# Order of state terms, scans and own terms in the first attention items of a fused RWKV-5 and mixture-of-experts kernel

## The chip, the cores and the metric

The kernel runs on one core of one Trainium2 chip, in float32. The metric is the device time in microseconds (us) of one execution; of several runs the median is taken. A core has five engines with instruction queues of their own, each worked off in order: TensorE (PE; its weight loads are listed apart as PEld), VectorE (DVE), ScalarE (ACT), GpSimd (POOL) and SyncE (SP, which here only issues DMAs).

## What is computed

A recurrent attention block feeds a mixture of experts with one expert for each token:

```python
# attention: B=4, H=8, S=768, head size 48
for t in range(S):
    kt, vt, rt = (k[:, :, t], v[:, :, t], r[:, :, t])
    cur = np.einsum('bhd,bhe->bhde', u[None] * kt, vt)
    y[:, :, t] = np.einsum('bhd,bhde->bhe', rt, state + cur)
    state = w[None, :, :, None] * state + np.einsum('bhd,bhe->bhde', kt, vt)
# x = y as (B, S, 384); experts: E=8, hidden 1024
logits = x @ w_gate;  local_gate = sigmoid(x @ w_local)
e = argmax(logits[b, s]) if s == 0 or local_gate[b, s] < 0.5 else prev_e
out[b, s] = softmax(logits[b, s])[e] * (np.maximum(x[b, s] @ w1[e], 0.0) @ w2[e])
```

## The kernel before

The attention is cut into 16 items (n = 0 to 15), each a batch b = n // 4 and a pair of heads; the sequence of an item is cut into six chunks of 128 tokens. Counted from one, the change's "item 4" is n = 3. Within a chunk the output is a masked matrix product; across chunks it goes through a state. An item consists of these steps, each a method of `Attention`:

- `load(n)`: three DMAs on SP's queue (rk: r and k; kv: k and v by token; vT). It is issued three items ahead; rk and vT have four buffers each, kv has five.
- `scale(n)`: POOL makes ke (keys weighted with the decay to the chunk's end), pd (r times k) and, from n = 3 on, rw (r times the decay). The order is pd, ke for n < 3; rw, ke, pd later; ke, rw, pd for n = 4.
- `keys(n)`: DVE makes kw (keys divided by the decay), and rw for n < 3.
- `added(n)` (L253): 20 matmuls write what each chunk adds to the state into T, 240 columns of the PSUM tile mp. There is one T for all items, and mp also serves the router.
- `states(n)` (L259): one DVE scan turns T into the states S.
- `scores(n, g)` (L288): 24 matmuls into one of two PSUM pairs, g = 0 and 1 being halves of the chunks. It returns the DVE step (L290) that multiplies by the mask into am. The pairs are handed out in turn to scores, to `turn` and to the logits.
- `own(n)` (L269): 8 matmuls write each token's own term into the PSUM tile y (one buffer, released when ScalarE has copied the previous item's y to xT, L314), and DVE multiplies it by vT (L273).
- `inside(n)` (L297) adds the masked products to y, `before(n)` (L310) adds the states' terms and copies y out.
- `turn(n)` (L323, L325) transposes xT into the token layout x; behind the last pair of heads of a batch x is stored to DRAM (L328), for the experts' gathers.

Everything is under a schedule written out by hand: `run` emits the steps in the order in which each engine works them off. Iteration n emits the inside and state terms of item n - 1. For n = 1 and 2 it then emits the scores of item n, both halves, then own, added and states. From n = 5 on the scores run one item ahead (`ahead = n + 1`), n = 4 does its own and those of n = 5. Added and states of item n come early in iteration n, for n = 4 on; for n = 3 they come at the end of its own iteration:

```python
self.scores(ahead, 0)()
keep = self.scores(ahead, 1)
# n == 3, shortened to what it runs
self.own(n)
self.added(3)
keep()
self.states(3)
```

The router of the experts works on two groups of two batches. Its steps for group 0 are laid between the items: with g = 8, `experts_of` in n = 9, `keys` and `runs` (transpose of the key into mp, scan over it) in n = 10, `turn_runs`, `last` and `one_hot` in n = 11, `counts` and `ranks` in n = 12, `slots` in n = 13. Those for group 1 lie between the hidden blocks of the first expert (`Experts.routing`). `one_hot` makes the expert's index ei[:, 1] and, with a shift by 9 on DVE (L720), its multiple of 512 in ei[:, 2], which `slots` adds (L780). The weights of the first expert are fetched on SP's queue in n = 14 (`fetch`, L1039 and L1041), behind all loads of the attention.

Of the kernel before, what the change touches and what calls it, by code (L numbers as in the profile page):

```python
# [11 lines left out]
F32 = mybir.dt.float32  # L12
I32 = mybir.dt.int32
# [7 lines left out]
P = 128  # L21
# [11 lines left out]
ST = 4  # L33
# [28 lines left out]
class Attention:  # L62
# [254 lines left out]
    def turn(self, n, banks):  # L317

        nc, b, h0 = self.nc, self.items[n]["b"], 2 * self.items[n]["hp"]
        xT, x = self.xTs[b], self.xs[b]  # L320
        for h in range(2):
            for c2 in range(C2):
                nc.tensor.transpose(banks[h][:, c2 * P:c2 * P + U], xT[:U, h0 + h, c2 * P:(c2 + 1) * P], self.ident[:U, :U])  # L323
        for h in range(2):
            nc.scalar.copy(x[:, :, (h0 + h) * DH:(h0 + h + 1) * DH],  # L325
                           banks[h][:, :C2 * P].rearrange("p (c e) -> p c e", e=DP)[..., :DH])
        if h0 == H - 2:
            nc.scalar.dma_start(out=self.x_d[b * S:(b + 1) * S, :].rearrange("(c p) d -> p c d", p=P), in_=x)  # L328

    def logits(self, b, bank):  # L330

# [13 lines left out]
    def run(self, router, fetch, heads):  # L345
# [11 lines left out]
        for n in range(M + 1):  # L357
            if n + AHEAD - 1 < M:
                self.load(n + AHEAD - 1)
            elif n + 2 == M:  # L360
                fetch()
            if n == 0:
                self.scale(0)
                self.keys(0)
                self.tables()
                self.scores(0, 0)()
                self.scores(0, 1)()
                self.own(0)
                self.nc.scalar.copy(self.first, self.tab[:, 1, 0])
                self.turn_ends(slice(1, HP))  # L370
                self.warm(3)
                self.added(0)
                self.reciprocals(1)
                self.states(0)
                self.scale(1)
                continue
            if n < 3:

                self.keys(n)
                self.inside(n - 1)  # L380
                self.before(n - 1)
                if n == 2:
                    self.turn(0, pair("tp"))
                self.nc.scalar.copy(self.first, self.tab[:, n + 1, 0])
                self.scores(n, 0)()
                keep = self.scores(n, 1)
                self.own(n)
                keep()
                self.added(n)
                self.states(n)  # L390
                if n == 1:
                    self.reciprocals(2)
                self.scale(n + 1)
                continue
            if n < M:
                self.turn(n - 2, pair("tp"))
                if n == 3:
                    self.reciprocals(3)
                if n < 5:
                    self.keys(n)  # L400
                if n > 3:
                    self.added(n)
                    self.states(n)
            if n == 4:
# [24 lines left out]
            self.before(n - 1)  # L429
            if n == 6:  # L430
                router.cast()
            if n == M:
                break
            if n == g + 3:
                router.last(0, mp[:, mp_end:])
                router.one_hot(0, (0,))
            if n == g + 7:

                router.summed(0, 0)
                router.copied(0, self.nc.vector.tensor_copy)  # L440
                router.head(pair("tb")[0])
                heads()

            ahead = n if n < 5 else n + 1
            if ahead < M:
                self.scores(ahead, 0)()
                keep = self.scores(ahead, 1)
            if n % HP == 0:

                keep()  # L450
                self.own(n)
                self.logits(n // HP - 1, pair("lp")[0])
                if n == 4:
                    self.scores(5, 0)()
                    self.scores(5, 1)()
                    self.keys(6)
                if n == g + 4:
                    router.counts(0, [mp, mp[:, E * NC // 2:]])
                    router.ranks(0, (0,))
                if n > 4:  # L460
                    self.keys(n + 2)
                if n == g + 4:
                    router.ranks(0, (1,))
            else:
                self.own(n)
                if n == g + 2:
                    router.keys(0, mp)
                    router.runs(0)
                if n == 3:
                    self.added(3)  # L470
                if 4 < n < M - 2:
                    self.keys(n + 2)
                if ahead < M:
                    keep()
                if n == 3:
                    self.states(3)
            if n == g + 1:
                router.experts_of(0, (1,))
            if n == g + 3:
                router.one_hot(0, (1,))  # L480
            if n == g + 5:
                router.places(0, 0)
            if n == g + 6:
                router.places(0, 1)
# [82 lines left out]
class Router:  # L567
# [27 lines left out]
    def open(self, i, pool):  # L595
        g, c = self.g[i], self.g[i]["nc"]
        for name, shape, dt in (
                ("mx", [P, c], F32), ("eq", [P, c, E], F32), ("k", [P, c], F32), ("key", [P, c], F32),
                ("run", [c, P], F32), ("rn", [P, c], F32), ("inc", [P, c + 1], F32),
                ("ei", [P, 3, c], I32), ("oh", [P, E, c], F32),  # L600
                ("exc", [P, E, c + 1], F32), ("pos", [P, E, c], F32), ("far", [P, EARLY, c], F32),
                ("r", [P, c], F32), ("si", [P, 3, c], I32),
                ("eqv", [P, c, E * ST], F32), ("val", [P, c, E * ST], F32), ("ohq", [P, c, P], F32),
# [105 lines left out]
    def one_hot(self, i, parts=(0, 1)):  # L709
# [7 lines left out]
        if 1 in parts:  # L717
            nc.vector.tensor_tensor(g["oh"], spread(g["ei"][:, 1], 1, E), spread(self.ie, 2, g["nc"]), op=Alu.is_equal)

            nc.vector.tensor_scalar(g["ei"][:, 2], g["ei"][:, 1], 9, None, Alu.arith_shift_left)  # L720

    def counts(self, i, bank):

# [52 lines left out]
    def slots(self, i):  # L776

        nc, g = self.nc, self.g[i]
        nc.vector.tensor_reduce(g["r"], g["pos"].rearrange("p e c -> p c e"), axis=AX.X, op=Alu.add)
        nc.vector.scalar_tensor_tensor(g["si"][:, 0], g["r"], float(ST * P - 1), g["ei"][:, 2], Alu.min, Alu.add)  # L780
        nc.vector.tensor_scalar(g["si"][:, 1], g["si"][:, 0], P - 1, None, Alu.bitwise_and)
        nc.vector.tensor_scalar(g["si"][:, 2], g["si"][:, 0], 7, None, Alu.arith_shift_right)

# [937 lines left out]
```

## Time and profile before

| what | us |
|---|---|
| median of 3 runs (lowest, highest) | 386.14 (385.8, 387.54) |
| the profiled execution | 384.17 |
| its span, first to last instruction | 382.4 |
| granted TensorE clock, mean | 0.995 |

Busy time and DMA by stage of that execution (us, but for the last two columns; the stages are cut near where PE starts the scores of n = 1, 2, 3, 4 and 6, then at the router's first transpose and the first logits of the last batch):

| stage | length | PE | DVE | ACT | POOL | DMA share | GB/s |
|---|---|---|---|---|---|---|---|
| 0 to 14.0 | 14.0 | 12.21 | 10.45 | 5.03 | 10.69 | 0.85 | 312 |
| 14.0 to 20.8 | 6.8 | 6.14 | 6.08 | 1.62 | 4.72 | 1.03 | 410 |
| 20.8 to 27.4 | 6.6 | 6.14 | 5.65 | 2.06 | 5.67 | 1.03 | 413 |
| 27.4 to 34.8 | 7.4 | 5.65 | 5.84 | 1.18 | 7.40 | 1.02 | 408 |
| 34.8 to 44.3 | 9.5 | 9.16 | 6.54 | 2.18 | 9.50 | 1.02 | 411 |
| 44.3 to 75.0 | 30.7 | 30.70 | 24.64 | 9.59 | 28.32 | 0.98 | 359 |
| 75.0 to 111.0 | 36.0 | 32.83 | 28.46 | 9.29 | 20.41 | 0.62 | 220 |
| 111.0 to 382.0 | 271.0 | 264.01 | 161.59 | 76.23 | 63.82 | 0.41 | 145 |

How to read it: a stage whose PE column is shorter than its length has idle PE time; the share of DMA is the mean over 16 DMA engines, and a share at 1 means that all had packets under way throughout. Attention is over at about 111 us; behind it lie the ten blocks of the experts. Lines of the profile are those of the kernel's file: `L253` is the matmul of `added`.

### The profile page before, as it was taken

Reading aid. Unit: us, or ns where it says so; the run is one execution under the profiler, and the core shown is the slowest. Engines: PE = TensorE matmul, PEld = TensorE weight load, DVE = VectorE, ACT = ScalarE, POOL = GpSimd, SP = SyncE. Lnnn points to the kernel's source line nnn. Section 1 sums busy time; section 2 is a strip of 40 time slices with the busy share of each in tenths; the row PEclk is TensorE's granted clock in tenths of the full one; section 3 lists DMA queues with packets and bytes.
Section 4 is the critical chain, followed back from the end, with each engine's and each line's share of the span. In section 5 each row is a group of like instructions: output and inputs, shape, how many; then the busy total and the mean of one; then the engine's idle time right before and its main releaser. Section 6 shows DMA issues by size and latency. Waiting matters only on the chain. (4 is left out here: it accounts for less than half of the span.)

```text
span 382.4 us, 9699 instructions
## 1 busy us (share of the span) xinstructions
PE 366.8 (96%) x3858; PEld 324.6 (85%) x3858; DVE 249.3 (65%) x719; ACT 107.2 (28%) x292; POOL 150.5 (39%) x212
## 2 busy tenths in 40 slices
PE   8998999998999999999999999999999999999992
PEld 7775777786759998999999999999998899899971
DVE  6888678888934746496566857758758758466400
ACT  4131233222222112322322333233234233232210
POOL 7779999787222042311422313212323113012022
PEclk9999999999999999999999999999999999999998
DMA  7999998989216881820561254145246156064011
GB/s 267 410 411 411 404 377 311 372 308 351 100 33 204 319 353 30 315 109 22 207 207 62 54 195 195 53 173 207 76 166 228 37 178 228 12 215 169 2 37 37
DMA packets 17477, 74.97 MB, mean 196 GB/s; under 512 B 2729, under 2 KB 6586, under 8 KB 14864
## 3 DMA queue, kind: packets, MB, share of 16 engines
q1 hardware_dynamic: 10048, 56.89, 39.9%
q0 software_dynamic: 3424, 9.52, 7.4%
q10 hardware_dynamic: 3952, 7.87, 5.7%
q8 instruction: 32, 0.52, 0.5%
q14 instruction: 21, 0.17, 0.1%
HBM read 64.83 MB, written 9.51 MB: 194 GB/s over the span
## 5 line engine op out<-in xcount | busy, mean ns | idle before, releaser
L1278 POOL DMA_INDIRECT out_dram<-yo,sid x27 | 26.6, 987 | 102.4 <-ACT yo L1273 79.0
L1129 PE MATMUL h<-exT,w1t 128*128 128x168 f32 (+4 forms) x240 | 54.9, 327 | 0.0
L1133 DVE TENSOR_TENSOR hT<-h,hs 128x168 f32<-128x168 f32 (+3 forms) x60 | 21.1, 351 | 46.4 <-PE h L1129 30.4
L1052 POOL DMA_INDIRECT xg<-x_d,gid x29 | 31.1, 1074 | 37.4 <-DVE sm L887 17.4
L1129 PEld LDWEIGHTS h<-exT,w1t 128*128 128x128 f32 x240 | 41.6, 190 | 0.3 <-issue 0.3
L1079 PE MATMUL h<-exT,w1t 128*128 128x192 f32 (+1 forms) x192 | 38.2, 337 | 0.0
L1198 PE MATMUL y<-factors,sums 128*128 128x192 f32 x168 | 36.8, 326 | 0.0
L290 DVE TENSOR_TENSOR am<-pair,kept 128x768 f32<-128x768 f32 x32 | 30.0, 951 | 8.3 <-PE pair L288 8.1
L1129 PE MATMUL h<-xs,ws 128*128 128x168 f32 (+4 forms) x144 | 35.2, 326 | 0.0
L221 POOL TENSOR_TENSOR pd<-rk 128x384 f32<-128x384 f32 x32 | 31.4, 1003 | 9.6 <-PE y L269 7.4
L1079 PEld LDWEIGHTS h<-exT,w1t 128*128 128x128 f32 x192 | 32.3, 190 | 1.4 <-issue 0.2
L1129 PEld LDWEIGHTS h<-xs,ws 128*128 128x128 f32 x144 | 25.5, 190 | 4.3 <-ACT hs L1136 1.2
L1198 PEld LDWEIGHTS y<-factors,sums 128*128 128x128 f32 x168 | 28.9, 190 | 0.0
L297 PE MATMUL y<-am,kv 128*64 128x128 f32 x384 | 25.1, 276 | 1.0 <-DVE y L273 1.0
L217 POOL TENSOR_TENSOR ke<-kv,endT 128x288 f32<-128x288 f32 x32 | 24.9, 797 | 1.9 <-POOL rw L234 0.8
L234 POOL TENSOR_TENSOR rw<-rk,tab 128x384 f32<-128x384 f32 x26 | 23.6, 928 | 1.4 <-DMA rk<-in_rk_dram 1.4
L288 PE MATMUL pair<-rw,kw 48*64 48x128 f32 (+1 forms) x768 | 22.6, 249 | 0.8 <-DVE kw L241 0.4
L1198 PE MATMUL y<-w2t,hT 128*128 128x192 f32 x96 | 23.0, 328 | 0.0
L314 ACT COPY xT<-y 128x768 f32<-128x768 f32 (+1 forms) x16 | 12.5, 779 | 37.1 <-PE y L310 37.1
L297 PEld LDWEIGHTS y<-am,kv 128*64 128x64 f32 x384 | 21.1, 137 | 1.9 <-DVE y L273 1.3
L1066 DVE COPY exT<-tp 128x384 f32<-128x384 f32 (+6 forms) x29 | 14.0, 489 | 12.9 <-PE tp L1065 12.6
L288 PEld LDWEIGHTS pair<-rw,kw 48*64 48x64 f32 x768 | 19.4, 133 | 3.0 <-issue 0.9
(280 smaller groups left out, 734.7 us busy)
## 6 DMA issues: line engine op xcount, KB each, us to landing
w1t<-in_w_dram SPq DMA_DIRECT2D x9, 1536.0 KB, 6.6
w2t<-in_w_dram SPq DMA_DIRECT2D x9, 1536.0 KB, 7.2
rk<-in_rk_dram SPq DMA_DIRECT2D x15, 768.0 KB, 8.4
kv<-in_kv_dram SPq DMA_DIRECT2D x16, 584.0 KB, 8.7
vT<-in_vT_dram SPq DMA_DIRECT2D x16, 384.0 KB, 6.7
x_d<-x ACTq DMA_DIRECT2D x4, 1152.0 KB, 9.6
w1t<-in_w_dram ACTq DMA_DIRECT2D x1, 1536.0 KB, 10.6
w2t<-in_w_dram ACTq DMA_DIRECT2D x1, 1536.0 KB, 13.8
```

Source lines behind the costliest of these rows:

```text
L217: nc.gpsimd.tensor_mul(t["ke"][:, p::2], t["k"][:, p::2], spread(self.endT[:, p, hp], 1, C2))
L221: nc.gpsimd.tensor_mul(t["pd"][:, z], t["rT"][:, z], t["kT"][:, z])
L234: engine.tensor_mul(t["rw"][:, z], t["rT"][:, z], spread(pw, 1, z.stop - z.start))
L288: nc.tensor.matmul(sc[f * DP:(f + 1) * DP, h, i, x:], lhsT=t["kw"][q, c, o * DP:(o + 1) * DP], rhs=t["rw"][q, c, x:], start=True, stop=True)
L290: return lambda: nc.vector.tensor_mul(t["am"][:, g], sc, spread(self.kept[:, g:g + 3], 1, 2))
L297: nc.tensor.matmul(t["y"][p * DP:(p + 1) * DP, h, c2 * P:(c2 + 1) * P], lhsT=t["v"][:, (2 * c + h) * DH:(2 * c + h) * DH + DP], rhs=t["am" ...
L1052: self.nc.gpsimd.indirect_dma_start(out=xg[:n], out_offset=None, in_=self.x_d[:rows], in_offset=bass.IndirectOffsetOnAxis(ap=u["gid"][:n, ...
L1079: nc.tensor.matmul(h[:, :n], lhsT=u["w1"][:, m, kk, :], rhs=u["xT"][:, kk, :], start=(kk == 0), stop=(kk == DK - 1))
L1129: nc.tensor.matmul(out, lhsT=a, rhs=b, start=start and k == 0, stop=stop and k == len(terms) - 1, skip_group_check=True)
L1133: nc.vector.tensor_tensor(out, a, b, op=Alu.add)
L1198: return lambda: nc.tensor.matmul(bank[:, x * half:(x + 1) * half], lhsT=a, rhs=b, start=(j == 0 and x == 0), stop=(j == FK // 2 - 1), ski ...
L1278: self.nc.gpsimd.indirect_dma_start(out=out.rearrange("n (h d) -> (n h) d", h=2) if half else out, out_offset=bass.IndirectOffsetOnAxis(ap ...
```

## The change

- In iterations n = 1 and 2, `own(n)` moves between the two halves of the scores; DVE's order (mask, own product, mask) stays as it was.
- Iteration n = 3 gets an ending of its own: added and states of n = 3 first, then the first half of the scores, own, and the second half.
- `added(5)` moves from iteration 5 into iteration 4, between the halves of the scores of n = 5. `added(11)` moves from iteration 11 into iteration 10, behind `own(10)` and ahead of the router's transpose into mp. Their scans (`states`) stay where they were.
- The store of x of batch 2 is issued on SP's queue, not on ScalarE's.
- `one_hot`'s shift on DVE becomes a multiplication by 512 on ScalarE, with a float result eb; `slots` adds eb. This holds for both groups.

```diff
         if h0 == H - 2:
-            nc.scalar.dma_start(out=self.x_d[b * S:(b + 1) * S, :]...
+            (nc.sync if b == 2 else nc.scalar).dma_start(out=self.x_d[b * S:(b + 1) * S, :]...
...
                 self.scores(n, 0)()
-                keep = self.scores(n, 1)
                 self.own(n)
-                keep()
+                self.scores(n, 1)()
                 self.added(n)
                 self.states(n)
...
                 if n > 3:
-                    self.added(n)
+                    if n not in (5, g + 3):
+                        self.added(n)
                     self.states(n)
...
             ahead = n if n < 5 else n + 1
+            if n == 3:
+                self.added(3)
+                self.states(3)
+                self.scores(3, 0)()
+                self.own(3)
+                self.scores(3, 1)()
+                continue
...
                 if n == 4:
                     self.scores(5, 0)()
+                    self.added(5)
                     self.scores(5, 1)()
...
                 self.own(n)
                 if n == g + 2:
+                    self.added(n + 1)
                     router.keys(0, mp)
                     router.runs(0)
-                if n == 3:
-                    self.added(3)
...
-                if n == 3:
-                    self.states(3)
...
-            nc.vector.tensor_scalar(g["ei"][:, 2], g["ei"][:, 1], 9, None, Alu.arith_shift_left)
+            nc.scalar.activation(g["eb"], g["ei"][:, 1], Act.Copy, scale=float(ST * P))
...
-        nc.vector.scalar_tensor_tensor(g["si"][:, 0], g["r"], float(ST * P - 1), g["ei"][:, 2], Alu.min, Alu.add)
+        nc.vector.scalar_tensor_tensor(g["si"][:, 0], g["r"], float(ST * P - 1), g["eb"], Alu.min, Alu.add)
```

More of the change, by code (lines that the diff above doesn't have):

```diff
@@ L327, in turn @@
         if h0 == H - 2:
-            nc.scalar.dma_start(out=self.x_d[b * S:(b + 1) * S, :].rearrange("(c p) d -> p c d", p=P), in_=x)
+            (nc.sync if b == 2 else nc.scalar).dma_start(out=self.x_d[b * S:(b + 1) * S, :].rearrange("(c p) d -> p c d", p=P), in_=x)
     def logits(self, b, bank):
@@ L599, in open @@
                 ("run", [c, P], F32), ("rn", [P, c], F32), ("inc", [P, c + 1], F32),
-                ("ei", [P, 3, c], I32), ("oh", [P, E, c], F32),
+                ("ei", [P, 2, c], I32), ("eb", [P, c], F32), ("oh", [P, E, c], F32),
                 ("exc", [P, E, c + 1], F32), ("pos", [P, E, c], F32), ("far", [P, EARLY, c], F32),
```

## The prediction

> **What bounds the kernel now.** I read the page first (busy shares, slices), then the waits of TensorE (PE), then the timelines of PE, VectorE (DVE) and GpSimd (POOL) in the stages that the diff touches. Busy shares, and the head of PE's own waits over the whole span (us in total, times, longest):
>
> ```profile
> PE 366.8 (96%) x3858; PEld 324.6 (85%) x3858; DVE 249.3 (65%) x719; ACT 107.2 (28%) x292; POOL 150.5 (39%) x212
> ```
>
> ```profile
> PE mp L253 <- POOL pd L221: 1.7, 1, 1.7
> PE pair L152 <- POOL ident masks.py:199: 1.5, 1, 1.5
> PE y L297 <- DVE y L273: 1.0, 2, 0.5
> PE mp L253 <- DMA w1t<-in_w_dram: 0.9, 1, 0.9
> PE pair L323 <- DVE am L290: 0.7, 2, 0.3
> ```
>
> PE is the bound; from 111 us on (the experts) no wait of PE at all is listed, so what is won or lost in the attention goes to the end unchanged. The waits listed lie in the attention, and the largest stands in the item that the change rewrites. (The second is the start of the program; the fourth, at 91.31, names a load that lands at 92.4 and isn't read there: the router's sum that reads mp until 91.06 fits better, and the change leaves it.) PE's timeline (start, length, line, tiles, idle before):
>
> ```profile
> 16.23 0.66 PE L253 MATMUL mp<-kv,ke 128*48 128x48 f32 x20
> 17.43 1.95 PE L297 MATMUL y<-am,kv 128*64 128x128 f32 x24 [0.54 <-DVE y L273]
> ...
> 27.43 1.24 PE L288 MATMUL pair<-rw,kw 48*64 48x128 f32 x48 [0.39 <-DVE kw L241]
> ...
> 29.82 0.79 PE L323 MATMUL pair<-ident,xT 112*128 112x112 f32 x6
> 32.34 0.66 PE L253 MATMUL mp<-kv,ke 128*48 128x48 f32 x20 [1.72 <-POOL pd L221]
> 32.79 1.53 PE L297 MATMUL y<-am,kv 128*64 128x128 f32 x24
> ```
>
> and DVE's at the same places:
>
> ```profile
> 16.41 0.97 DVE L273 TENSOR_TENSOR y<-y,vT 128x768 f32<-128x768 f32 x1 [0.49 <-PE y L269]
> ...
> 28.27 0.96 DVE L290 TENSOR_TENSOR am<-pair,kept 128x768 f32<-128x768 f32 x1 [0.66 <-PE pair L288]
> 29.85 0.97 DVE L273 TENSOR_TENSOR y<-y,vT 128x768 f32<-128x768 f32 x1 [0.63 <-PE y L269]
> 30.73 0.95 DVE L290 TENSOR_TENSOR am<-pair,kept 128x768 f32<-128x768 f32 x1
> 31.59 0.64 DVE L259 TENSOR_TENSOR_SCAN S<-step,mp 128x240 f32<-128x240 f32 x1
> ```
>
> Three things are to be seen. The terms of n = 4 (32.34) overwrite T, which the scan of n = 3 (ending 32.23) must have read; the profile names POOL's pd, which ends at 32.25, but the matmuls read only ke and v. So I take the scan as the releaser. Second, that scan is last in a DVE chain (mask, own product, mask, scan) that idles 0.66 + 0.63 us for PE. Third, n = 1 has the same idle piece (0.49) before DVE's own product, and PE pays for it at 17.43.
>
> **A rule of the skill beside the trace.** The Trainium skill, "SBUF — State Buffer", section "Who interferes with whom", says that a DVE tensor_scalar can enter a mode that needs the port pair shared with GpSimd, and then blocks for the whole of a GpSimd instruction that has it. The trace agrees for the shift that the change takes off DVE:
>
> ```profile
> 84.22 1.98 POOL L234 TENSOR_TENSOR rw<-rk,tab 128x384 f32<-128x384 f32 x2
> 85.26 0.97 DVE L720 TENSOR_SCALAR ei<-ei 128x12 int32<-128x12 int32 x1
> 86.15 0.64 DVE L259 TENSOR_TENSOR_SCAN S<-step,mp 128x240 f32<-128x240 f32 x1
> 87.69 1.50 PE L336 MATMUL pair<-xT,wp 128*32 128x384 f32 x16 [0.29 <-DVE am L290]
> ```
>
> Twelve columns take 0.97 us and end with POOL's second rw (86.20); the same shift in the second group takes 0.17 us. The forecast goes by the 0.97.
>
> **Part by part.**
>
> *n = 1 (own terms ahead of the second scores).* Own needs pd (13.75), the first scores (14.85) and y, which ScalarE's copy frees at 14.80. So own runs 14.88 to 15.7 in place of 15.40 to 16.3. The DVE product follows the first mask without idling: 15.83 in place of 16.41, **0.58 us** earlier, and mask, scan, Newton step and keys of n = 2 with it. PE's inside terms (17.43, stretched to 1.95 against 1.5 elsewhere as they wait for the second mask) end at about 18.85, not 19.38: 0.55. If ScalarE's copy came 0.1 late, 0.1 of this goes.
>
> *n = 2.* Same move: own at 21.05 in place of 22.23, product at 22.05 in place of 23.24, and the second mask ends at 23.9, where before inside started at 24.37. Inside then runs 1.5 in place of 1.83. PE finishes its state terms L310 at 26.25, not 27.03: 0.78 in all, 0.2 more than n = 1 gave.
>
> *n = 3.* Now added(3) is first (26.2 to 26.85; ke ready at 24.26), covering the keys' wait (0.39, and the keys are ready at 26.1 anyway). The scan runs 26.95 to 27.6, scores at 26.8, own at 27.5 (pd ready 26.19; y freed 27.1), second scores to 29.05. DVE: first mask 27.65, product 28.5, second mask 29.4 to 30.3. PE: turn(2) to 29.8, added(4) to 30.4 with T long free, inside(3) at 30.4 when the second mask is in. Before: 32.79. The 1.72 us stall goes, and **late next is the second mask**, which PE just meets. Sum up to here: **2.4 us** (0.55 + 0.2 + 1.65).
>
> Does POOL keep up? It runs without a gap from 26.87 (there it waited for kv(4)) and is not moved. PE would want ke(4) at 29.75 (ready 28.43), pd(4) at 33.75 (32.25), rw(5) at 36.0 (34.28), ke(5) at 36.7 (35.80), rw(6) at 42 (39.93). The smallest cover is 0.9 us. Later POOL waits for PE (2.37 us at 70.06), so it has just that much in hand.
>
> *added(5) between the scores of n = 5.* 0.6 us of PE work is moved from behind turn(3) to before it. Turn(3) waited 0.34 us for a bank, and this fills that; but the second scores end at 40.5 (old clock), their mask at 41.5, and the token logits take that mask's bank: they start at 41.57, before 41.55. Gain **0**; from -0.1 to +0.3.
>
> *added(11) behind own(10).* Before, it waited 0.44 us until run's scan (ends 76.59) had read mp, though other columns: the tile is tracked whole. Moved, it runs at 75.1, and inside(10) starts 0.45 sooner. Yet turn_runs then waits for the scan of n = 11 (ends 78.86) at the same 78.92, since DVE is busy without a gap from 70.9. Gain **0**. What it is moved past is the key's transpose, which ends at 76.0; DVE gets to it at 76.19, so 0.2 us of cover; without it, up to 0.4 lost.
>
> *Shift on ScalarE.* For group 0 the scan of n = 12 and the masks after it come 0.9 us sooner; the logits' wait for a bank (0.29, and PE's issue a little) goes, own(12) is late next: **-0.3**. ScalarE is idle there from 80.83 to 82.93; its casts of such a size took 0.2 us. For group 1 ScalarE waits for ei (124.37) with the Relu of the next block queued behind; eb is done at about 124.6 and that Relu started at 124.84: 0, with 0.2 of cover.
>
> *Store of x(2) on SP.* ScalarE loses one DMA issue of 0.38 us at 91.15 and then waits for PE anyway: 0. On SP all loads are out by 83.23, but w1 and w2 of the first expert (83.61, 84.71) now stand behind a store that waits for x(2) at about 88.5. Before, they landed in 8.8 and 12.6 us. 4.3 MB at the 410 GB/s seen early on is 10.4 us, so I estimate landing by 101, against a first use at 112.8 (115.49 before). Twelve us of cover, 0.
>
> **Sum:** -2.4 - 0.3 = **-2.7 us**. The profiled execution took 384.17 (span 382.4, 1.77 outside): 381.5. The three runs' median is 386.14, 2.0 above it; the same difference gives **383.4**. Bounds of the sum: -1.9 (a late copy, 0.3 each for the two moved terms) to -3.2.
>
> **Rivals.**
>
> *B, added(4) is really held by POOL.* The profile names pd, and pd(4) ends 0.09 us before the start. Nowhere does added(n) start before pd(n) ends, so the trace doesn't exclude it. For it: the name. Against: pd is no operand, and own(0) started at 8.99 while ke(0) was still to come, so single POOL instructions do release PE. Then PE stands at 32.3 as before and only the 0.3 is left: **385.8**.
>
> *C, POOL becomes the bound.* If its chain is 1 to 1.5 us later than in the old trace (phases against DVE shift), the head gain is cut to 1.2: **384.9**.
>
> *D, slower.* The loads keep 16 DMA engines wholly busy from 14 to 44 us (share 1.02 at 410 GB/s), and POOL waits for two of them (rk(3) at 21.06, kv(4) at 26.87). Earlier DVE steps free vT and rk sooner, and SP issues the loads of n = 5 and 6 up to 0.8 us sooner, into the same engines, where they could push kv(4) back. PE then stands in order before added(4) and own(4). It decides from kv(4) later by the 1.3 us of cover, and costs more than it brings from 3.7 us (1.3 + 2.4); at 5 us late, **387.1**. Against it: loads of one queue are issued in order, and 0.8 us of transfer is the most that can be pushed in.
>
> **How the numbers follow.** Forecast 0.68, B 0.15, C 0.07, D 0.10. A measurement of this kernel can tell about 0.5% (1.9 us) from no change, so faster is below 384.2. Of the forecast's 0.68 some 0.07 falls above it, of C half below: faster 0.64, within 0.5% 0.26, slower 0.10. The runs spread by 1.7 us, the forecast's own range is 382.4 to 384.5; the range reaches B and below the forecast's best end: 381.9 to 386.2.
>
> **What would show it.** Right: no wait before L253 near 30 us, inside(3) at about 30.4; DVE's product of n = 1 at 15.8; no 0.29 before L336 of n = 12; a new wait of some 0.7 before turn_runs (L700) in place of 0.44 before L253; w1 landing before 102. Wrong: added(4) still at 32.3 (B), waits on POOL between 30 and 45 (C), kv(4) landing after 28 (D), or hidden blocks waiting for w1 or for a Relu queued behind eb.

## The result and the profile after

The changed kernel takes 388.01 us (median of 22 runs, 385.92 to 391.22); the kernel before, run beside it, takes 386.2 (385.05 to 387.78). The ratio is 1.0044, with a 95% interval of 1.0028 to 1.0061. So it is 1.7 us **slower**, where 2.7 us faster had been forecast. Its profiled execution took 389.49 us, 1.5 above that median, with a span of 387.7; that of the kernel before took 384.17, 2.0 below its own (span 382.4). So the two traces lie 5.3 us apart, three times what the medians do, and what they show has to be weighed with that.

The runs fall into two groups by TensorE's mean granted clock. In eight of the 22 it is 0.994 or more, and their median is 386.5; in the other fourteen it is 0.980 to 0.993, and theirs 388.5. Of 218 runs of the kernel before, made beside the experiments, 141 are in the upper group.

Busy time, from the page:

```profile
PE 369.5 (95%) x3858; PEld 327.3 (84%) x3858; DVE 248.8 (64%) x717; ACT 107.4 (28%) x294; POOL 150.6 (39%) x212
```

PE does the same 3858 matmuls and is busy 2.7 us *longer*: that is no wait, but matmuls that ran slowly, 1.7 of it by a stretch at half clock (below). Its waits (us in total, times, longest):

```profile
PE pair L288 <- issue: 4.2, 5, 1.1
PE pair L152 <- POOL ident masks.py:199: 1.5, 1, 1.5
PE mp L253 <- DVE pos L742: 1.2, 1, 1.2
PE mp L705 <- DVE inc L718: 0.9, 1, 0.9
...
PE pair L342 <- DVE am L290: 0.4, 1, 0.4
```

The 1.7 us before `added(4)` and the 0.39 before the scores are gone, as meant. In their place stands a wait that was not there: five pieces, 4.2 us, in the middle of scores, with **no releaser** ("issue": nothing that the profile shows), and a sixth in own(2). PE's timeline of the changed kernel, from own(2) to item 5 (start, length, line, tiles, idle before):

```profile
22.29 0.55 PE L269 MATMUL y<-pd,w_t 48*64 48x384 f32 x4 [0.27 <-issue]
...
27.25 0.66 PE L253 MATMUL mp<-kv,ke 128*48 128x48 f32 x20
27.83 0.44 PE L288 MATMUL pair<-rw,kw 48*64 48x128 f32 x6
28.80 0.60 PE L288 MATMUL pair<-rw,kw 48*64 48x64 f32 x17 [0.53 <-issue]
...
31.31 0.66 PE L253 MATMUL mp<-kv,ke 128*48 128x48 f32 x20
31.80 1.52 PE L297 MATMUL y<-am,kv 128*64 128x128 f32 x24
...
35.20 1.11 PE L288 MATMUL pair<-rw,kw 48*64 48x64 f32 x41 [0.94 <-issue]
...
41.35 0.44 PE L288 MATMUL pair<-rw,kw 48*64 48x128 f32 x8 [1.14 <-issue]
41.72 0.79 PE L323 MATMUL pair<-ident,xT 112*128 112x112 f32 x6
42.95 0.84 PE L342 MATMUL pair<-sel,lT 128*128 128x18 f32 x6 [0.44 <-DVE am L290]
43.73 2.38 PE L297 MATMUL y<-am,kv 128*64 128x128 f32 x24
```

`added(4)` (31.31) no longer stalls and `inside(3)` starts at 31.80, 0.99 before its old 32.79. (This trace is 0.35 late already at the first scores of n = 1; the table under e17 counts from there.) But the scores of n = 4 then stop for 0.94, and those of n = 5, cut apart at 41.35, for 1.14. `inside(4)` at 43.73 is 1.41 *behind* its old 42.32. It also takes 2.38 us in place of 1.53. The stages of that stretch (length; busy us and instructions of PE, PEld, DVE, ACT, POOL; granted clock, DMA share, GB/s):

```profile
40.00:44.00 4.00, 2.42 (x35) 1.87 (x29) 2.23 (x4) 0.87 (x3) 4.00 (x7) 1.00 1.02 411
44.00:48.00 4.00, 4.00 (x74) 3.67 (x74) 0.92 (x20) 0.43 (x2) 3.35 (x7) 0.57 1.03 382
```

PE idles 1.58 us of four, and in the next four the clock is halved (0.57). In the profile of the kernel before PE is busy 3.76 us from 40 to 44, and no slice of the attention has a lowered clock. DVE did what was forecast (compare the timeline of before: mask, product, mask, scan with 0.66 + 0.63 idle):

```profile
27.95 0.65 DVE L259 TENSOR_TENSOR_SCAN S<-step,mp 128x240 f32<-128x240 f32 x1 [0.30 <-PE mp L253]
29.49 0.96 DVE L290 TENSOR_TENSOR am<-pair,kept 128x768 f32<-128x768 f32 x1 [0.89 <-PE pair L288]
30.37 0.95 DVE L273 TENSOR_TENSOR y<-y,vT 128x768 f32<-128x768 f32 x1
31.23 0.94 DVE L290 TENSOR_TENSOR am<-pair,kept 128x768 f32<-128x768 f32 x1
```

The scan is ahead and the chain runs through; only the first mask comes 1.8 us later than forecast (29.49 against 27.65). The scores in front of it start 1.0 later than forecast (27.83 against 26.8), and they stop for 0.53. `added(4)` starts at 31.31, in the middle of POOL's pd(4), so it does not wait for that:

```profile
30.90 1.97 POOL L221 TENSOR_TENSOR pd<-rk 128x384 f32<-128x384 f32 x2
```

The router's stage:

```profile
81.98 0.23 PE L705 MATMUL mp<-ident,run 12*128 12x12 f32 x1 [0.92 <-DVE inc L718]
90.13 0.32 PE L288 MATMUL pair<-rw,kw 48*64 48x128 f32 x4 [0.55 <-issue]
91.14 1.50 PE L336 MATMUL pair<-xT,wp 128*32 128x384 f32 x16
94.98 0.66 PE L253 MATMUL mp<-kv,ke 128*48 128x48 f32 x20 [1.15 <-DVE pos L742]
105.32 0.90 PE L288 MATMUL pair<-rw,kw 48*64 48x128 f32 x31 [1.01 <-issue]
```

The wait before `turn_runs` came (0.92), the logits' 0.29 went, but `added(13)` now waits 1.15 in place of 0.93, and there are two more stops without a releaser. In the experts, 0.9 us more goes in this execution, with a wait of 0.64 for ScalarE's hT at 148.59. It is not the change's: the traces of e10 and e12 below, with the order of before, have it, and those of e5 and e8 don't.

**What the stops are.** They stand at fixed numbers of PE instructions. Counting weight loads, matmuls and semaphore instructions from the start, they lie at 705, 961, 1217, 1473, ..., 256 apart, whatever line is there. The page has a DMA queue `q8 instruction` with 32 packets and 0.52 MB, so 16 KB each: blocks of PE's own program (its 7830-odd instructions make 31 blocks of 256), which pass through the same 16 DMA engines as the loads. From the records of those packets and of PE (us; "delay" from the entry into a block to the start of the packet that carries the next one; "slack" from the packet's end + 1.4 to the entry into that next block; 1.4 is what lies between the packet's end and PE's next instruction at the stops):

```
                    before                      changed
count     entered  delay  slack       entered  delay  slack
  449       14.89   3.16   1.14         15.50   4.28  -0.01
  705       21.73   3.41   0.27         22.29   3.99  -0.01
  961       27.93   3.47   1.08         28.80   3.83   0.06
 1217       34.99   3.59   0.07         35.20   3.68   0.02
 1473       41.09   2.80   0.60         41.35   3.30   2.90
 1729       46.92   1.69   1.38         49.99   0.90   2.03
```

I read this so: PE asks for the next block about when it enters one. (The trace shows no request. In the experts' part of the kernel before, where the DMA engines are busy 0.37 of the time, packets start up to 1.85 us ahead of the entry as counted here, so the request comes somewhat before it.) The packet queues 3 to 4.3 us behind loads, takes 1.0 to 1.1, and 1.4 later PE can go on: 5.7 to 6.8 us for a block, nearly the length of an item (252 PE instructions). PE alone needs some 5.2 (in the kernel before the three blocks from 46.92 to 62.59). In the kernel before the waits of the items stood beside this and left 0.07 to 1.1 us of slack. Take them away and PE stands at the next block: four entries in a row with no slack at all, and the packets come 0.1 to 1.1 us later after the entry than before. I call this theory **F** (the fetch of instructions). Its rival **O** is that the order of the steps itself makes the time, with the stops as a by-product.

### The profile page after: what moved, and what is told of

Read it like the earlier page. It is cut to its first block, busy times and chain, and to the rows that moved or that the text cites. A ratio compares the mean times of both kernels' runs of the same rounds, so it can differ in the third digit from the quotient of the medians.

```text
span 387.7 us, 9700 instructions
## 1 busy us (share of the span) xinstructions
PE 369.5 (95%) x3858; PEld 327.3 (84%) x3858; DVE 248.8 (64%) x717; ACT 107.4 (28%) x294; POOL 150.6 (39%) x212
## 5 line engine op out<-in xcount | busy, mean ns | idle before, releaser
L221 POOL TENSOR_TENSOR pd<-rk 128x384 f32<-128x384 f32 x32 | 31.5, 1005 | 12.4 <-PE y L269 10.2
L288 PE MATMUL pair<-rw,kw 48*64 48x128 f32 (+1 forms) x768 | 25.3, 252 | 4.7 <-issue 4.2
L288 PEld LDWEIGHTS pair<-rw,kw 48*64 48x64 f32 x768 | 21.3, 135 | 7.9 <-issue 5.6
L1071 DVE COPY exT<-tp 128x384 f32<-128x384 f32 (+6 forms) x29 | 14.0, 488 | 13.8 <-PE tp L1070 13.5
## 6 DMA issues: line engine op xcount, KB each, us to landing
w2t<-in_w_dram SPq DMA_DIRECT2D x9, 1536.0 KB, 13.8
```

The costliest lines, as they stand in the source:

```text
L221: nc.gpsimd.tensor_mul(t["pd"][:, z], t["rT"][:, z], t["kT"][:, z])
L288: nc.tensor.matmul(sc[f * DP:(f + 1) * DP, h, i, x:], lhsT=t["kw"][q, c, o * DP:(o + 1) * DP], rhs=t["rw"][q, c, x:], start=True, stop=True)
```

## The experiments

"hx" below stands for the three edits of n = 1 to 3 (own amid the scores in n = 1 and 2, the ending of n = 3), as in the change's diff. Every ratio is to the kernel before on the same chip, with its 95% interval.

### Parts of the change

**e1_head_only**: the kernel before + hx.

> Kernel before with the head's reordering alone: own between the scores in n = 1 and 2, and n = 3 with added and scan first. Theory F (fetch): PE takes its instructions in blocks of 256 through the DMA engines that the loads keep full; on entering a block the next is asked for, and it is there some 6.3 us later, where the block itself could run in 5.3. Then the head can't get shorter: within 1 us of before, and gaps without a releaser (issue) inside the scores near 22, 29 and 35 us take the place of the 1.72 us stall. Theory O (order): the loss of the whole change comes from the waits that the moved added(5) and added(11) make by their place, and the head works as predicted: faster than before by 2 us or more.

385.94 us, ratio 0.9986 (0.9965 to 1.0007). PE's timeline has the same stops at the same counts, 961 and 1217 among them:

```profile
28.51 0.60 PE L288 MATMUL pair<-rw,kw 48*64 48x64 f32 x17 [0.53 <-issue]
...
34.64 1.11 PE L288 MATMUL pair<-rw,kw 48*64 48x64 f32 x41 [0.67 <-issue]
```

The reordered items alone bring some 0.5 us, not 2.4; O's gain is not there.

**e8_head_eb**: e1 + the shift on ScalarE (L720, L780).

> The head's reordering with the shift on ScalarE, without the moved added(5), added(11) and store. Both theories: the shift's 0.3 us at the logits is paid back at the router's scan over the counts, whose two inputs lie in SBUF and which ends 0.2 us behind POOL's first rw in both traces; so as e1, within 0.5 us of it.

385.13 us, 0.9997 (0.9981 to 1.0013): nothing. The shift adds no gain. Its trace has `added(13)` waiting 1.31 us in place of 0.93, because the router's scan of counts (`exc`, both inputs in SBUF) now takes 0.96 us in place of 0.58. It starts at 91.39 against POOL's rw at 91.27, and ends just after the first half of that rw; before, it started at 90.11, half a microsecond into the rw of 89.59, and ended at the same point of it. That fits another rule of the section named in the prediction (the Trainium skill, "SBUF — State Buffer", "Who interferes with whom"): a DVE instruction with two SBUF inputs contends with a GpSimd instruction that reads SBUF. Where POOL's rw of one item had held the shift, that of the next item holds another DVE instruction.

**e5_added5_only**: the kernel before + `added(5)` moved.

```diff
-                    self.added(n)
+                    if n != 5:
+                        self.added(n)
...
                     self.scores(5, 0)()
+                    self.added(5)
                     self.scores(5, 1)()
```

> Kernel before with added(5) alone moved between the scores of n = 5. After e1 and e3 theory F says: the wait for the block of instructions and the wait for the mask then lie one behind the other (in the kernel before they overlap), PE idles about 2 us of 3.4 near 41 us, and in most runs the clock is halved for one or more stretches of 3.4 us behind it. So slower by 1.5 to 3 us with a mean clock of 0.989 to 0.991 in the median run, as in e4. Rival: the loss needs the reordered head in front of it as well; then this is within 0.5 us of before.

386.24 us against 385.39, 1.0022 (1.0004 to 1.0039): slower by 0.9 us, less than expected, and the median clock is 0.994, as in the kernel before, not 0.989 to 0.991. The profiled execution, with 390.93 us the longest of 23, has the clock halved behind these steps and again near 85 us. The scores are cut in this order too, ahead of that:

```profile
40.82 0.44 PE L288 MATMUL pair<-rw,kw 48*64 48x64 f32 x9 [0.54 <-issue]
42.42 0.84 PE L342 MATMUL pair<-sel,lT 128*128 128x18 f32 x6 [0.44 <-DVE am L290]
```

The kernel before, at the same place:

```profile
38.37 1.53 PE L288 MATMUL pair<-rw,kw 48*64 48x128 f32 x48
40.24 0.79 PE L323 MATMUL pair<-ident,xT 112*128 112x112 f32 x6 [0.34 <-DVE am L290]
...
41.55 0.84 PE L342 MATMUL pair<-sel,lT 128*128 128x18 f32 x6
42.32 1.53 PE L297 MATMUL y<-am,kv 128*64 128x128 f32 x24
```

There the wait for the mask's bank (0.34) stood before `turn(3)`, and the block of count 1473 arrived meanwhile. With `added(5)` in that place the block stops the second scores, and the token logits (L342), which take the bank of their mask, wait 0.44 on top. The two waits lie one behind the other: from the first scores of n = 5 to the logits it is 3.99 us in e5 (42.42 - 38.43), 3.18 before. The 0.44 comes from the order, not from the stop: it stands in e9, e14 and e17 below, where no stop cuts these scores.

**e3_added5_back**: the changed kernel with `added(5)` in iteration 5 again.

> Kernel after with added(5) in iteration 5 again. Theory F: a gap of about 1 us stays near 41 us, as PE enters the block at the same count of instructions, but it falls into other work; the wait for the mask's bank (0.44) goes, and with less idle PE time perhaps the stretch at half clock (3.4 us long, 1.7 us lost): 0.5 to 2 us faster than after. Theory O: the bank wait goes and the gap too: about 1.5 us faster than after, and no gap near 41 us.

386.65 us, 1.0001 (0.9984 to 1.0018), 1.4 below the changed kernel (1.7 by the ratios). PE still stops at count 1473, for 0.33 and inside `added(5)`, as F says. So moving `added(5)` is the larger part of the loss.

**e4_added11_back**: the changed kernel with `added(11)` in iteration 11 again.

> Kernel after with added(11) in iteration 11 again. Theory F: PE waits 0.4 before added(11) in place of 0.9 before the runs' transpose; 0 to 0.5 us faster than after. Theory O: the 0.9 us wait goes whole: 0.9 us faster than after.

388.63 us, 1.0049 (1.0024 to 1.0074), the same as the changed kernel: this move costs and brings nothing. Its trace has a stretch of 10.2 us at half clock from 42.6 on, behind the changed kernel's two waits (1.14 and 0.44).

**e2_store_act**: the changed kernel with the store of x(2) on ScalarE's queue.

```diff
-            (nc.sync if b == 2 else nc.scalar).dma_start(out=self.x_d[...
+            nc.scalar.dma_start(out=self.x_d[...
```

> Kernel after with the store of x(2) on ScalarE's queue again. Theory F: the store and the two weight loads no longer fall on the block that PE enters near 98.7 us; the gap of 1.0 us in the scores near 105 us is gone, and about 1 us of the time with it (387 us where after has 388). Theory O: the store has twelve us of cover, no change against after.

388.91 us, 1.0052 (1.0031 to 1.0073): the median doesn't come down to the 387 that F expected. The trace, though, shows what the store does. On SP, w1 and w2 are issued at 95.04 and 95.63 (before 83.61 and 84.71), so that they fill the engines when PE asks for the block of count 4033 (98.66): its packet starts 4.3 us later and PE stops for 1.01 at 105.32. From `added(13)` to the inside terms of n = 15 it is 18.88 us in the changed kernel (94.98 to 113.86), 18.13 in e2, and 18.14 before. So the store costs 0.7 us in that profile; in the medians it can't be seen beside the spread.

### Block ends moved

Small transposes and matmuls in the idle time at the start are exchanged, so that 48 PE instructions fewer (e9 to e11) or more (e13 to e15) come ahead of the items. The order of the steps is untouched; a block end falls 48 instructions later or earlier in an item.

```diff
         self.align(26)
         self.warm(8)
...
-        self.align(26)
-        self.warm(8)
+        self.align(10)
+        self.warm(16)
```

**e9_after_shifted**: the changed kernel.

> Kernel after, with 16 of the 26 small matmuls at the start (line 152, four PE instructions each) replaced by 8 transposes of the same length in all (two each): 48 instructions fewer ahead of everything. Theory F: the blocks end 48 instructions later in the program, so the gaps at counts 705, 961, 1217, 1473 come at the same counts but in other work; at 1473 it falls into inside(4), behind the mask and the logits, so the bank wait of 0.44 and the doubled idle time go. The clock of the median run rises from 0.989-0.990 to 0.993 or more and the time falls by 1 to 2 us, to within 1 us of before. Theory O (the loss lies in the order of the steps, wherever the blocks end): as after, slower than before by 1.7 us.

388.84 us, 1.0074 (1.005 to 1.0099). The stops keep to the counts and stand in other work (1473 in `inside` now), as F says; the gain that F expected of it did not come: the blocks 961 and 1217 were later still (delays of 4.4 to 5.2), the wait of 0.44 for the mask's bank stayed, and the median clock of the six runs is 0.987, not 0.993 or more.

**e10_before_shifted**: the kernel before.

> Kernel before with the same shift by 48 instructions, the control of e9. Theory F: the slack at the block ends moves to other places, and the time by up to 1.5 us either way. Theory O: within 0.5 us of before.

386.71 us, 1.0011 (0.9993 to 1.0029), as expected.

**e11_head_eb_shifted**: e8.

> e8 (reordered head and shift on ScalarE) with the same shift. Theory F: the head stays at 6.3 to 6.5 us for a block whatever the order, so within 1 us of e8; it is the candidate for a version faster than before.

388.16 us, 1.0045 (1.0023 to 1.0067): by the ratios 1.9 us above e8 (which ran on another chip, so that the 3.0 between the medians doesn't count), with every step in the same order. Two of its stops, in other places than those of e8:

```profile
35.40 0.60 PE L288 MATMUL pair<-rw,kw 48*64 48x64 f32 x17 [1.40 <-issue]
...
43.10 1.36 PE L297 MATMUL y<-am,kv 128*64 128x128 f32 x21 [0.66 <-issue]
```

All blocks from 961 to 2753 are late here, with delays of 3.5 to 5.2 us. So the order of the steps doesn't set the time by itself; where a block end lies against the loads does.

**e13_head_eb_other_shift, e14_after_other_shift, e15_before_other_shift**: 48 instructions more (`align(42)`, `warm(0)`), on e8, the changed kernel and the kernel before.

> The reordered first items and the shift on ScalarE alone, with 48 more TensorE instructions in the idle time at the start (32 small matmuls... in place of 8 larger transposes), so that every block of 256 instructions ends 48 instructions earlier in the items than in head_eb (there 385.1, ratio 0.9997). Theory F (a late block of instructions is what comes after the removed waits): the blocks are asked for earlier against the issue of the loads; if the 3 us that the opposite shift cost is read as a slope, this one brings 1 to 3 us: 382 to 384, ratio 0.992 to 0.997, with slack at two or more of the counts 705 to 1473. If the place doesn't matter but for the opposite shift's bad luck: 384.5 to 385.8 and zero slack at all of 705 to 1473 as before. Theory O (the order of the steps alone): the same 384.5 to 385.8, and gaps in the same places of the program (second half of the scores) as in head_eb.

> The whole change with the same 48 more instructions ahead. F: the scores of n = 5, which the block end 1473 cuts in the changed kernel (gap 1.14 us, then a wait of 0.44 for the mask's bank), are no longer cut there: the end lies 48 instructions earlier, in the steps ahead of them. Then the idle 2 us that go before the half clock are broken up, and the time is 384 to 387 (changed kernel 388.0), ratio 0.994 to 1.001. O: 387 to 389, as the order is the same, with the bank wait of 0.4 still there and half clock after it.

> The kernel before with the same 48 more instructions ahead, as the control: F: its own waits cover the blocks up to 47 us in either place, so 385.5 to 387, ratio 0.998 to 1.003. O: the same.

386.84, 388.07 and 387.13 us; ratios 1.0034 (1.0018 to 1.005), 1.0061 (1.0039 to 1.0084) and 1.0043 (1.0015 to 1.0071). All three are above what F expected; e14 fell where O had put it (387 to 389). The stops moved, at 961 and 1217 into `added` and `before`; in e14 the scores of n = 5 were no longer cut, but the mask's bank was waited for all the same:

```profile
39.69 0.39 PE L253 MATMUL mp<-kv,ke 128*48 128x48 f32 x8 [0.92 <-issue]
...
41.94 1.10 PE L342 MATMUL pair<-sel,lT 128*128 128x18 f32 x6 [0.44 <-DVE am L290]
42.97 2.83 PE L297 MATMUL y<-am,kv 128*64 128x128 f32 x24
```

With the start's idle time made up otherwise, even the kernel before loses 0.4%: its place was a good one. No shift made any of the three faster.

### Loads added and taken away

**e6_before_ahead3, e7_after_ahead3**: three buffers ahead, not four (`AHEAD = 3`), meant to shorten the queue of loads.

> Kernel before with three buffers for rk and vT and four for kv in place of four and five, so that a load is issued when a buffer comes free one item later and fewer bytes stand in the queues. Theory F: blocks of instructions arrive sooner in the head (less than 3 us from entering a block to the packet's start, where it was 3.2 to 3.6), which the kernel before doesn't need: same time within 1 us, unless POOL then waits for loads, which would cost up to 2 us. Theory O says nothing of it but the latter.

> Kernel after with the same fewer buffers. Theory F: with shorter queues the gaps inside the scores near 22, 29, 35 and 41 us shrink or go, the second scores of n = 5 and their mask are no longer late, and the clock stays at 0.995; then it is faster than e6 by 1 to 2.5 us. Theory O (the loss lies in the order of the steps): as much slower than e6 as after is than before, 1.5 to 2 us.

385.79 us, 1.0016 (0.9998 to 1.0034), and 387.79 us, 1.004 (1.0018 to 1.0063). In e7 the stops at 705, 961 and 1217 stay (e6, like the kernel before, has none there), and it is 2.0 us above e6, as O had it and F had not. With a buffer less the engines are as full up to 28 us (share 1.02 in both) and nearly so to 44 (0.92 against 1.02). It didn't empty the queue, so I take it to tell nothing between F and O.

**e12_before_more_loads**: the kernel before, with eight copies of 384 KB from DRAM to DRAM, whose result nothing reads, beside the items 6 to 9.

```diff
+            if 6 <= n < 10:
+                for i in range(2):
+                    self.nc.scalar.dma_start(out=self.more[2 * n + i - 12], in_=self.w1[0, :, 768 * i:768 * i + 768])
```

> Kernel before with eight copies of 384 KB each from the first expert's weights to unused memory, two in each of n = 6 to 9, issued on ScalarE's queue; nothing reads them. PE has no wait there in the kernel before, and blocks arrive 0.6 to 1.2 us ahead of their use. Theory F: with the engines fuller the packet of a block starts 3 us or more after PE enters the block before (1.1 to 2.3 without), and gaps without a releaser appear at counts 1985, 2241 or 2497, 0.3 to 1.5 us each; slower by 1 to 3 us. Rival: instructions have a path of their own, or the gaps have another cause; then no gap appears at these counts, and the time changes only by what late loads cost, under 1 us, as loads are more than one item ahead.

389.93 us, 1.0114 (1.0075 to 1.0154). Where the kernel before has delays of 1.1 to 2.3 us (counts 1985 to 2497), they are now 3.5 to 3.7, at 3009 5.8, and PE stops at the counts 2241, 2497, 3009 and 3265:

```profile
58.60 0.61 PE L253 MATMUL mp<-kv,ke 128*48 128x48 f32 x19 [0.63 <-issue]
64.66 1.13 PE L336 MATMUL pair<-xT,wp 128*32 128x384 f32 x9 [0.70 <-issue]
77.08 0.28 PE L288 MATMUL pair<-rw,kw 48*64 48x128 f32 x3 [0.64 <-issue]
...
85.40 0.43 PE L288 MATMUL pair<-rw,kw 48*64 48x128 f32 x8 [1.18 <-issue]
```

The order of PE's steps is that of the kernel before. The loads make the stops.

**e16_before_few_loads, e17_after_few_loads, e18_head_eb_few_loads**: the kernel before, the changed kernel and e8 without the loads of kv for n = 5 to 9 and of vT for n = 4 to 9; these items compute with the data of an earlier one.

```diff
-        nc.sync.dma_start(out=kv, in_=self.kv_d[b, hp])
-        nc.sync.dma_start(out=vT...
+        if not 5 <= n < 10:
+            nc.sync.dma_start(out=kv, in_=self.kv_d[b, hp])
+        if not 4 <= n < 10:
+            nc.sync.dma_start(out=vT...
```

> The kernel before, with vT of items 4 to 9 and kv of items 5 to 9 not loaded (the buffers keep the data of an earlier item): from about 17 us on the loads are less than half. F: the blocks of instructions come 1 to 2.3 us after they are asked for, not 3 to 3.6, and lie 1 us and more ahead of their use from 20 us on; the waits of the kernel before stay (0.54 at 17.4, 0.39 at 27.4, 1.72 at 32.3, the last shorter if POOL's pd, which waits for kv(4), had a part in it). Time 384.5 to 386 against 385.5 to 386.2. O: the same, and the packets' delay without meaning.

> The changed kernel with the same loads left out. F: the gaps at the block ends 961, 1217 and 1473 go (0.6, 1.1 and 1.3 us between starts), the scores of n = 5 aren't cut, and what the prediction forecast for the head appears: count 1473 is reached 1.5 to 2.7 us sooner than in the kernel before with the same loads (counted from count 449), median 382 to 384.5, 1.5 to 3 us below that kernel. O (the order itself loses): the gaps in the scores and the wait of 0.4 for the mask's bank stay, and the median is 1 to 2.5 us above that kernel.

> The reordered items 1 to 3 and the shift on ScalarE alone, with the same loads left out. F: 1.5 to 3 us below the kernel before with the same loads, and the same as or below the whole change with them; slack of 0.5 us and more at the counts 705 to 1473. O: within 1 us of the kernel before with the same loads.

With wrong data in these items the experts' part takes far longer, probably because the routing falls out otherwise: 2772.02, 2769.84 and 2770.5 us in all (four runs each). So only the differences count: by the medians the whole change is **2.2 us faster** than the kernel before, e8 1.5. The runs' ranges overlap a little (2771.35 to 2776.74 and 2768.74 to 2771.6), so I go by the traces. PE in e17, at the places shown above (two lines further down in the file):

```profile
28.37 0.60 PE L290 MATMUL pair<-rw,kw 48*64 48x64 f32 x17 [0.53 <-issue]
...
31.37 1.53 PE L299 MATMUL y<-am,kv 128*64 128x128 f32 x24
...
33.47 1.27 PE L290 MATMUL pair<-rw,kw 48*64 48x128 f32 x46
...
40.29 0.84 PE L344 MATMUL pair<-sel,lT 128*128 128x18 f32 x6 [0.43 <-DVE am L292]
41.06 1.53 PE L299 MATMUL y<-am,kv 128*64 128x128 f32 x24
```

The DMA engines have idle time from about 28 us on (share 0.62 from 28 to 36). The block ends 705 and 961 are fetched before that and still stop PE; at 1217 and 1473 it no longer stops. `inside(4)` takes 1.53 us at full clock. The wait for the mask's bank (0.43) stays, as O had it: from the first scores of n = 5 to the logits it is 3.34 us against 3.17 in e16, so without a stop in front it costs 0.17. Gains over the kernel before with the same loads, each counted from the first scores of n = 1 in its own trace (us; negative is a loss):

```
reached                  forecast   changed - before   e17 - e16
inside(1)                  0.55          0.28             0.48
before(2), L310            0.78          0.06             0.25
inside(3)                  2.4           1.34             1.51
count 1217                 2.4           0.14             1.51
inside(4)                  2.4          -1.06             1.34
added(13)                  2.7          -3.32             1.96
inside(15)                 2.7          -4.06             1.49
```

The same change, with the same order, gains 1.5 to 2 us where the loads are fewer and loses where they are not. That is F, and it ends O for the reordered items. (It is one trace each. Up to `inside(4)` traces of the same order agree to 0.3 us; further down less, e1 and e8 lie 1.7 apart at `inside(15)`.) From `added(13)` to `inside(15)` e17 loses 0.47 again, with a stop of 0.71 at count 4033: the store on SP. e18, without it, keeps its gain (18.13 us for the stretch, as in e16).

## Why the prediction was wrong

**What bounds the kernel.** That PE is the bound stands. But the page was read as if PE's waits for other engines were all that held it. The row `q8 instruction` was on the page of before and in no step of the sum.

**n = 1, -0.55.** Half came: own waits for ScalarE's copy of y (0.32), a cover the prediction had named as thin; 0.28 in the trace.

**n = 2, -0.2; n = 3, -1.65: "late next is the second mask".** This is the step that failed. For n = 2 the stop at count 705 stands in own itself, and the gain falls from 0.28 at inside(1) to 0.06 at before(2). The waits of 0.39 and 1.72 did go; `added(4)` ran while pd(4) was under way and did not wait once the scan was ahead, so the mechanism in DVE and POOL was read rightly and rival B is out. But late next was PE's own next block of instructions. The kernel before entered its blocks at 14.89 and 41.09, 26.2 us for four; the changed kernel takes 25.85, e1 25.58, each with no slack in any of the four: 0.35 to 0.6 of the 2.4 forecast. With the loads thinned, some two thirds of it appears (1.51), held back by the two blocks that still queue. Why the packets' delay grows just as the order gets tighter (3.2 to 3.6 us before, 3.7 to 4.3 after) the runs don't settle; that the blocks' place against the loads decides is shown, the rule behind it isn't.

**added(5), 0 (from -0.1 to +0.3).** It costs 0.9 us alone (e5) and 1.4 within the change (e3). The sum had the mask's bank wait (41.5 against 41.55) on the edge and no block end in the scores ahead of it. The first alone was nearly right: the wait costs 0.17 in e17, inside the range. But the idle piece that it "filled" had been covering the fetch. Behind it the clock can halve: a stretch of 3.41 us in the changed kernel's profile, worth 1.7. The mean clock of a run is 0.989 to 0.9905 in the median for e2, e4 and e14, which share this order, against 0.994 for the kernel before. But it is 0.994 in e5, which has the move too, and 0.992 in e3, which has not and whose trace has a stretch at half clock near 95 us, in the router's stage. So the move is not all that lowers the clock. This was in no bound of the range.

**added(11), 0.** Right, with `turn_runs` waiting 0.92 in its place as forecast.

**Shift on ScalarE, -0.3.** The bank wait of 0.29 went; "own(12) is late next" did not hold. `exc` grew from 0.58 to 0.96 and ended with the same POOL rw as before, so `added(13)` comes no sooner: from `turn_runs` to it 12.39 us both in the kernel before and in e2, the changed kernel without a stop in that stretch. Right about the port, wrong in not asking which DVE instruction POOL's next rw would hold.

**Store on SP, 0 with "twelve us of cover".** The weights were in time, though not by 101: the store went out at 94.59, not about 88.5, and w2 landed at about 109.4 (95.63 + 13.8), with the first use at 119.90. What they collided with was not: 0.7 us at count 4033 in the changed kernel's trace, 0.47 in e17's. The prediction asked what waits for these loads, not what must pass beside them.

**Rivals.** None was right. D had the right sign and the right resource, DMA engines busy at a share of 1.02, but the wrong victim: POOL starts ke(4) 0.25 us later, counted from the first scores of n = 1, and nobody waits for it. C is out, since no wait on POOL appears from 30 to 45 us.

**The sum, corrected.** By whole medians: head about -0.5 (e1), `added(5)` +0.9 to +1.4, the rest 0, as the store's 0.7 shows in traces alone: +0.4 to +0.9, beside +1.7 measured. The runs with a mean clock of 0.994 or more say where the rest lies (medians, us; "before" are such runs on the same chip):

```
                 such runs   median   before   difference
e1                19 of 22   385.81   386.23     -0.42
e8                 9 of 14   384.72   385.21     -0.49
e5                14 of 23   385.89   385.21     +0.68
e3                 7 of 22   385.78   386.23     -0.45
e2                 4 of 22   386.46   386.23     +0.23
e4                 5 of 22   386.73   386.23     +0.50
changed            8 of 22   386.50
```

Here the head's -0.4 and the +0.7 of `added(5)` make +0.3, and e2 and e4, each the change less one part, lie at +0.2 and +0.5. So I estimate 1.2 to 1.5 of the 1.7 to be the clock, which is lower in 14 of the changed kernel's 22 runs and in 77 of the 218 of before. The estimate picks runs by what happened in them, few in some rows, so it is no proof. Why the clock is lower more often is not settled. No version tried beats the kernel before; e8 and e1 are equal to it.

## What to carry to other kernels

Before a wait is forecast to vanish, ask what else is hidden beside it: a stream of instructions that is fetched through the same DMA engines as the loads has a least time per block, and where the engines are full that time, not the engine's own work, can be the next bound. Stops without a releaser at equal distances in the count of instructions are its mark; compare entry times over several blocks, and thin the loads to prove it. Sort the runs by granted clock before a difference of medians is given to a step. And never move work into a short idle piece without asking what arrives during it.

## What the runs showed of the hardware

- PE's program comes in blocks of 256 instructions (16 KB). Counted from the entry into a block, the packet of the next starts 1.1 to 2.3 us later where the loads leave a little room (kernel before, counts 1985 to 2497, DMA share 0.97), 3 to 4.3 where they fill the engines (share 1.02), up to 7.1 (e10, count 3521).
- The granted clock can halve without any long gap: 1.58 us idle in four, in pieces of at most 1.14, and then 3.41 us at half clock (10.2, three times that, in e4). The Trainium skill, "TensorE: Matmul & The Clock Gate", section "Why this matters for your kernels", advises against idle gaps beyond about 3 us; here shorter ones in a row were enough, in some executions and not in others: e2, with 1.56 us idle from 40 to 44, kept its clock. In e17 the same order, with PE busy 7.57 of 8 us from 36 to 44, kept its clock.
- A DVE scan with both inputs in SBUF took 0.58 us where it started 0.52 us into a POOL instruction that reads SBUF (before, 90.11), and 0.96 where it started 0.12 us into one (e8, 91.39).
